# Gathering the rows of three experts instead of two in quarters of 128 columns, turned by VectorE, in a retention and mixture-of-experts kernel

## The chip, the core and the metric

The kernel runs on one core of a Trainium2 chip. The metric is the device time of one execution in microseconds. TensorE multiplies matrices, VectorE and ScalarE work element by element, GpSimd does so too and also starts the indirect transfers (gathers and scatters), SyncE starts the plain loads. Each engine takes its instructions in the order in which they were written and waits at semaphores for the others.

## What is computed

Retention (attention with a decay in place of the softmax) over 8 batches, 8 heads, 576 positions and 64 channels gives 4608 tokens of 512 channels. Every token goes to one of 8 experts, at most 576 tokens to each, chosen greedily by the logits; an expert is two products with a ReLU between.

```python
ret = (0.125 * q @ k.transpose(0, 1, 3, 2)) * Dmat      # gamma_h ** (i - j) for i >= j, else 0
x = (ret @ v).transpose(0, 2, 1, 3).reshape(4608, 512)
flat = (x @ w_gate).flatten()
for idx in np.argsort(-flat):
    tok, e = idx // 8, idx % 8
    if assigned[tok] >= 0 or counts[e] >= 576: continue
    assigned[tok] = e; counts[e] += 1
for e in range(8):
    out[assigned == e] = np.maximum(x[assigned == e] @ w1[e], 0) @ w2[e]
```

## The kernel before

**Stages.** The first 165 us or so are the retention; its rows go to a scratch tensor `xd` in HBM. Then eight experts follow. They are handled in the order in which they fill up: I call the expert that is found p-th "expert p", from 0 to 7, and `e` in the code of the products is that p. For an expert, TensorE runs the first product (`l1`, line 1041, PSUM tile `ph`) and the second (`l2`, line 1082, `py`). Every float32 operand is split in a high and a low part (`xh` and `xl`, `w1h` and `w1l`), and three of the four partial products are kept.

**The first product** has 16 steps: 8 blocks `f` of the hidden channels, each with the tokens 0 to 255 (12 products of 256 columns) and then the tokens 256 to 575 (12 products of 320 columns). So its first step needs the gathered blocks of tokens 0 and 1, and its second step needs blocks 2, 3 and 4, low parts too. **The second product** has five token blocks: four of 24 products of 512 columns, and a fifth of 64 tokens with 16. Three of those 24 (one `f`) I call a triple, two of the 16 a pair.

**Search and listing.** While TensorE works for expert p, VectorE looks for expert p+1 and then p+2 (class `Route`). A search has seven rounds; each is one count on TensorE (nine small products, line 353) and one stretch on VectorE that begins at line 357 and ends, with a new table `G` (line 177), before the next count. Then come `members` (counts of line 421) and `listing` (counts of line 459), which gives the indices of the rows in `idx` (line 471). Expert 7 needs no search.

**Gathering**, for expert e+1 while expert e is in work, is done in one of two ways, by the constant `PIECES`:

- For e < PIECES: five gathers of whole rows of 512 channels (line 975), four of 128 tokens and one of 64. TensorE turns each block with four transposes (line 1007) into PSUM, ScalarE copies out the high part (line 1009), VectorE subtracts for the low part (line 1010).
- For e >= PIECES: `listing` also makes the table `quarter` (lines 476 to 480, seven operations on VectorE), and 18 gathers follow (line 965), one for each of 128 indices, that fetch a quarter row of 128 channels. VectorE turns a block in place of TensorE (`xz`, line 991, two buffers), ScalarE copies out the high part (line 993), VectorE subtracts (line 994). The loader takes the weights of the first product from `w1n`, the same numbers in another order of channels, and four loads of 512 KB stay four loads of 512 KB.

```python
while left and (all or state['piece'] <= mix.t):
    k, v = left.pop(0)
    nc.gpsimd.indirect_dma_start(out=t[:, k, :], ..., ap=quarters[e][:, v:v+1], axis=0)
    state['piece'] = mix.t + 1300
if not left:
    XG[e] = t
    state['arrives'] = mix.t + 6000
```

**What sets the order.** A `Mixer` keeps a clock of its own, in nanoseconds, while the program is written: each triple of `l2` advances it by 650, each three products of `l1` by 320 or 400, and each stretch of VectorE by a fixed price. The next count of the search is written when that clock says that VectorE is done. `gather` writes a quarter gather every 1300 of that clock, and the turning of the blocks starts, one block for each triple, when `arrives` is over. So what stands behind what on each engine is decided here, when the program is built.

**GpSimd's queue** also holds, for each expert, eight transfers `w1l` and `w2l` (line 950), each of which forms the low part of a quarter of the weights in memory and waits for ScalarE's copy (line 949), and five scatters of results (line 1059). There is one buffer `xg` for gathered rows.

Of the kernel before, what the change touches and what calls it, by code (L numbers as in the profile page):

```python
# [19 lines left out]
NP, HP, NB = 4, 4, 9  # L20
N, DM, E, FF = 4608, 512, 8, 1024
SLACK = 1.0
PIECES = 6

def consts_np():
    h = np.arange(H); g = (1.0 - 2.0 ** (-5.0 - h)).astype(np.float64)
# [59 lines left out]
class Route:  # L86
# [341 lines left out]
    def listing(s, p):  # L428
# [43 lines left out]
        if early:  # L472
            s.room(cn)
        if p >= PIECES:
            s.quarter = pool.tile([128, 20], I32, name="quarter", bufs=2)
# [414 lines left out]
def moe(tc, nc, P, R, xd, w1_d, w2_d, out, mix):  # L890
# [11 lines left out]
    def phases():  # L902
        for p in range(E):
# [9 lines left out]
            found.append(R.idx)  # L913
            if p >= PIECES:
                quarters[p] = R.quarter
# [5 lines left out]
    def dma_pump():  # L921

        while state['dma'] < min(state['conv'] + 4, 8*E):
# [3 lines left out]
            t = P['raw']()  # L927
            src = ((w1_d[0] if e < PIECES else w1_d[1]) if k < 4 else w2_d)
            nc.sync.dma_start(t, src[bass.ds(regs[e], 1), :, (k % 4)*1024:(k % 4)*1024+1024].rearrange("a p x -> (a p) x"))
# [25 lines left out]
    def gather(e, all=False):  # L955
        if e in XG or not ready(e):
            return
        if e >= PIECES:
            if e not in parts:
# [20 lines left out]
    def transposes(e):  # L980
# [4 lines left out]
        XH[e], XL[e] = xh, xl  # L985
        if e >= PIECES:
            low = []
# [26 lines left out]
    def l1(e, tr):  # L1014
# [5 lines left out]
        for i, (f, s) in enumerate(order):  # L1020
            wh, wl = [w.rearrange("p (f d m) -> p f d m", f=2, d=4)[:, f % 2] for w in W1[e, f // 2]]
            if i == 0 and e >= PIECES:
                for _ in tr:
# [186 lines left out]
```

## Time and profile before

| | us |
|---|---|
| median of 3 runs | 625.21 (624.79 to 626.15) |
| the profiled execution | 626.64, of it the span 624.5 from the first to the last instruction |
| second product of expert 4 (the gathering for expert 5) | 429.70 to 459.41 |
| first and second product of expert 5 | 459.41 to 486.25 and 486.25 to 512.66 |
| first and second product of expert 6 | 512.66 to 538.3 and 538.3 to 563.8 |

All times inside the execution count from the first instruction. The products of TensorE overlap, so a row's duration is longer than the step from its start to the next row's start; what a group of products costs is read from the starts. A row of the timeline that ends in square brackets names the idle time ahead of the instruction and what ended it.

### The profile page before, as it was taken

The numbers are of one execution on the slowest core, as the hardware profiler recorded it, in microseconds if no ns is written. First come the engines' busy times: TensorE is split into PE (matmuls) and PEld (weight loads), VectorE is DVE, ScalarE is ACT, GpSimd is POOL, SyncE is SP. The second block draws the span as 40 slices with busy tenths as digits, with TensorE's granted clock in tenths as the row PEclk, the third lists the DMA queues.
The fourth block names the chain that finished last, engine by engine and source line by source line (L and its number), as shares of the span: only waits on it lengthen the run. The fifth ranks groups of instructions, "written<-read, shape, count | busy, mean of one in ns | idle before, by whom it ended". The sixth has DMA issues, their size and how long they took to land.

```text
span 624.5 us, 14777 instructions
## 1 busy us (share of the span) xinstructions
PE 600.9 (96%) x5718; PEld 518.3 (83%) x5722; DVE 406.7 (65%) x1487; ACT 270.5 (43%) x464; POOL 250.6 (40%) x297
## 2 busy tenths in 40 slices
PE   7999998998989999999999999999999999999993
PEld 5888887866589779978987997798789889989982
DVE  4646776698899878977885885689478632222200
ACT  1344432332347355542662456156435536645410
POOL 4887375410422262251242243124314868831121
PEclk9999998999999999999999999999999999999998
DMA  9999799954559699796889399559938887995410
GB/s 323 409 376 342 230 399 305 333 153 137 163 165 215 185 222 245 188 245 190 173 227 241 93 243 225 173 128 231 236 108 183 206 254 188 236 257 118 77 50 27
DMA packets 53352, 132.70 MB, mean 212 GB/s; under 512 B 7394, under 2 KB 22626, under 8 KB 53282
## 3 DMA queue, kind: packets, MB, share of 16 engines
q1 hardware_dynamic: 37906, 80.10, 37.7%
q0 software_dynamic: 15232, 51.39, 37.3%
q8 instruction: 45, 0.74, 0.5%
q10 hardware_dynamic: 144, 0.26, 0.1%
q14 instruction: 25, 0.20, 0.1%
HBM read 80.35 MB, written 18.87 MB: 159 GB/s over the span
## 4 chain that ended last, share of the span: by engine, by line
PE 75%; DVE 9%; DMA 7%; issue 6%; SPq 1%; POOL 1%; ACT 1%; POOLq 0%; DVEq 0%
PE py L1082 28%; PE ph L1041 28%; PE sc L603 4%; PE px L647 3%; DMA xd<-raw 3%; DMA vin<-in_vk 2%; PE px L638 2%; PE pS L624 2%; PE pt L1007 2%; PE r L353 1%; PE pT L679 1%; DVE hb L1048 1%; PE r L459 1%; DVE f L361 1%; DMA raw<-in_w 1%
## 5 line engine op out<-in xcount | busy, mean ns | idle before, releaser
L1082 PE MATMUL py<-w2h,hb 128*128 128x512 f32 x576 | 187.4, 397 | 0.0
L1041 PE MATMUL ph<-xh,w1h 128*128 128x320 f32 (+1 forms) x512 | 152.0, 301 | 0.2 <-ACT xh L1009 0.2
L1041 PE MATMUL ph<-xl,w1h 128*128 128x320 f32 (+1 forms) x512 | 149.7, 296 | 0.0
L1041 PE MATMUL ph<-xh,w1l 128*128 128x320 f32 (+1 forms) x512 | 149.5, 296 | 0.0
L1082 PE MATMUL py<-w2l,hb 128*128 128x512 f32 (+1 forms) x320 | 125.3, 392 | 0.0
L1082 PEld LDWEIGHTS py<-w2h,hb 128*128 128x128 f32 x576 | 104.4, 188 | 21.6
L1041 PEld LDWEIGHTS ph<-xh,w1h 128*128 128x128 f32 x512 | 96.3, 189 | 1.3 <-ACT xh L1009 0.7
L1041 PEld LDWEIGHTS ph<-xl,w1h 128*128 128x128 f32 x512 | 96.4, 190 | 0.2
L1041 PEld LDWEIGHTS ph<-xh,w1l 128*128 128x128 f32 x512 | 96.3, 189 | 0.0
L1045 ACT ACTIVATE hb<-ph 128x256 fp32r<-128x256 f32 (+1 forms) x128 | 52.2, 408 | 99.5 <-PE ph L1041 98.8
L1059 POOL DMA_INDIRECT out_y<-yt,idx x40 | 40.5, 1013 | 111.4 <-ACT yt L1099 73.0
L1048 DVE SCALAR_TENSOR_TENSOR hb<-ph,hb 128x256 fp32r<-128x256 f32 (+1 forms) x192 | 58.3, 352 | 40.0 <-ACT hb L1045 39.4
L1082 PEld LDWEIGHTS py<-w2l,hb 128*128 128x128 f32 (+1 forms) x320 | 56.7, 177 | 13.3 <-DMA w2l<-raw 0.4
L612 DVE TENSOR_TENSOR am<-sc,cst 128x1024 f32<-128x1024 f32 x32 | 39.1, 1223 | 37.5 <-PE sc L603 37.5
L588 POOL TENSOR_TENSOR qin<-qin,cst 128x512 f32<-128x512 f32 (+1 forms) x48 | 47.2, 1010 | 40.0 <-DMA qin<-in_qk 36.0
L950 POOL DMA_DIRECT2D w2l<-raw x32 | 29.4, 918 | 84.2 <-ACT w2l L949 44.4
L1099 ACT ACTIVATE yt<-py 128x512 f32<-128x512 f32 x32 | 19.1, 598 | 92.7 <-PE py L1082 73.5
L627 ACT ACTIVATE st<-pS,cst 128x128 f32<-128x128 f32 x64 | 23.5, 368 | 80.3 <-PE pS L624 80.3
L975 POOL DMA_INDIRECT xg<-xd,idx x30 | 30.0, 1000 | 68.7 <-DMA raw<-in_w 36.1
L950 POOL DMA_DIRECT2D w1l<-raw x30 | 28.0, 959 | 43.3 <-ACT w1l L949 36.1
L603 PE MATMUL sc<-qin,kin 64*128 64x128 f32 x512 | 39.9, 299 | 2.0 <-POOL qin L588 1.8
L965 POOL DMA_INDIRECT xg<-xd,quarter x36 | 36.3, 1008 | 12.8 <-issue 9.4
(192 smaller groups left out, 939.5 us busy)
## 6 DMA issues: line engine op xcount, KB each, us to landing
raw<-in_w SPq DMA_DIRECT2D x56, 512.0 KB, 6.1
w2l<-raw POOLq DMA_DIRECT2D x32, 512.0 KB, 6.0
w1l<-raw POOLq DMA_DIRECT2D x30, 512.0 KB, 7.2
qin<-in_qk SPq DMA_DIRECT2D x14, 576.0 KB, 6.6
kin<-in_qk SPq DMA_DIRECT2D x14, 576.0 KB, 7.0
vin<-in_vk SPq DMA_DIRECT2D x14, 576.0 KB, 9.2
nin<-in_vk SPq DMA_DIRECT2D x14, 512.0 KB, 8.7
xd<-raw SPq DMA_DIRECT2D x36, 128.0 KB, 6.4
```

The source lines that it names most:

```text
L588: nc.gpsimd.tensor_tensor(x, x, e[:, None, :n].to_broadcast([128, (b-a)//n, n]), op=ALU.mult)
L603: nc.tensor.matmul(t[:, h, 128*j:128*j+128], blk(k, 4*g+j)[r], blk(q, 4*g+j)[r], start=(j == 0), stop=True, skip_group_check=True)
L612: nc.vector.tensor_tensor(a, SC[u, g].rearrange("p h (j q) -> p h j q", q=128), m1[:, u % HP, :, None, :].to_broadcast([128, 2, 4, 128]), ...
L627: nc.scalar.activation(s, p, AF.Copy, scale=ss[:, u % HP, c:c+1])
L950: nc.gpsimd.dma_start(lo, raw, accum_op=ALU.add)
L965: nc.gpsimd.indirect_dma_start(out=t[:, k, :], out_offset=None, in_=xq[:, :], in_offset=bass.IndirectOffsetOnAxis(ap=quarters[e][:, v:v+1] ...
L975: nc.gpsimd.indirect_dma_start(out=xg[:n, j, :], out_offset=None, in_=xd[:, :], in_offset=bass.IndirectOffsetOnAxis(ap=found[e][:n, j:j+1] ...
L1041: T.matmul(ps, w, x, start=(k == 0), stop=(k == 11))
L1045: A.activation(hb[:, f, c], ps, AF.Relu)
L1048: V.scalar_tensor_tensor(hb[:, f, to+a:to+b], ps[:, a:b], 0.0, hb[:, f, 256*s+a:256*s+b].bitcast(F32), op0=ALU.max, op1=ALU.subtract)
L1059: st = nc.gpsimd.indirect_dma_start(out=out[:, :], out_offset=bass.IndirectOffsetOnAxis(ap=found[e][:n, t:t+1], axis=0), in_=y[:n], in_off ...
L1082: T.matmul(ps[:m], a, w, start=(k == 0), stop=(k == last), skip_group_check=True)
```

## The change

The constant goes from 6 to 5, so that expert 5 too is gathered in 18 quarter gathers and turned by VectorE; experts 6 and 7 were so already.

```diff
-PIECES = 6
+PIECES = 5
```

Twenty transposes of TensorE, five copies and five subtractions from PSUM go; seven operations on `quarter`, five turnings `xz`, five copies and five subtractions from SBUF come, and 18 gathers stand for 5. Since the mixer's clock sees other prices, other things move too.

On VectorE, at the end of the second product of expert 4 and the start of the first product of expert 5, the sixth round of the search for expert 6 stood before like this (`yt` is the last block of results of expert 4, `hb` the hidden layer of expert 5):

```order
L357 SCALAR_TENSOR_TENSOR cs<-room,r 32x8
L359 TENSOR_TENSOR cs<-cs,r 32x8 x2
L361 TENSOR_TENSOR f<-r,cs 32x8 x4
L367 TENSOR_REDUCE mq<-f 128x1
L368 STREAM_TRANSPOSE tc<-mq 128x32
L369 TENSOR_REDUCE j<-tc 128x1
L334 TENSOR_SCALAR v<-u,j 128x72
L177 TENSOR_TENSOR G<-ct,v 128x36x16
L1102 TENSOR_TENSOR yt<-yt,py 64x512
L1048 SCALAR_TENSOR_TENSOR hb<-ph,hb 128x256
```

and stands now like this (`xg` are the gathered rows of expert 5, the first row is the low part of block 2, the last two are those of blocks 3 and 4):

```order
L994 TENSOR_TENSOR xl<-xz,xh 128x4x128
L357 SCALAR_TENSOR_TENSOR cs<-room,r 32x8
L359 TENSOR_TENSOR cs<-cs,r 32x8 x2
L361 TENSOR_TENSOR f<-r,cs 32x8 x4
L367 TENSOR_REDUCE mq<-f 128x1
L368 STREAM_TRANSPOSE tc<-mq 128x32
L369 TENSOR_REDUCE j<-tc 128x1
L334 TENSOR_SCALAR v<-u,j 128x72
L177 TENSOR_TENSOR G<-ct,v 128x36x16
L991 STREAM_TRANSPOSE xz<-xg 128x4x64
L994 TENSOR_TENSOR xl<-xz,xh 128x4x128
L994 TENSOR_TENSOR xl<-xz,xh 128x4x64
```

The turning of expert 5's rows stands around that round: four of the five blocks ahead of it, the turning of the fifth block and two low parts behind it.

On GpSimd, in the second product of expert 5, the last gathers for expert 6 stood before like this:

```order
L965 DMA xg<-xd,quarter 128x128 x2
L950 DMA w1l<-raw 128x1024
L965 DMA xg<-xd,quarter 128x128 x2
L1058 MEMSET spacer_2326 1x1
L1059 DMA out_y<-yt,idx 4608x512
L965 DMA xg<-xd,quarter 128x128
L950 DMA w1l<-raw 128x1024
```

and stand now like this:

```order
L965 DMA xg<-xd,quarter 128x128 x2
L950 DMA w1l<-raw 128x1024
L965 DMA xg<-xd,quarter 128x128 x2
L1058 MEMSET spacer_2326 1x1
L1059 DMA out_y<-yt,idx 4608x512
L965 DMA xg<-xd,quarter 128x128
L950 DMA w1l<-raw 128x1024
L965 DMA xg<-xd,quarter 128x128 x3
```

The last two gathers, those of block 4, and the last of block 3 stand now behind the fourth `w1l`, which used to follow all of them.

On TensorE, the five groups of transposes between the first triples of the second product of expert 4 are gone. The listing counts for expert 6 (line 459) stand 27 products later in the first product of expert 5: 87 of its 192 products followed them before, 60 do now. The seventh count of that search stands after 30 products of it, where it stood after 15.

## Rows read from the trace of the kernel before

**Rows 1.** The page: busy time of each engine, share of the span, instructions

```profile
PE 600.9 (96%) x5718; PEld 518.3 (83%) x5722; DVE 406.7 (65%) x1487; ACT 270.5 (43%) x464; POOL 250.6 (40%) x297
```

**Rows 2.** Timeline of TensorE, second product of expert 4: start us, us, instruction

```profile
429.70 0.63 PE L1082 MATMUL py<-w2h,hb 128*128 128x512 f32 x2
...
437.65 0.39 PE L353 MATMUL r<-oh,G 128*128 128x32 bf16 x9
...
444.79 0.39 PE L353 MATMUL r<-oh,G 128*128 128x32 bf16 x9
...
449.91 0.39 PE L353 MATMUL r<-oh,G 128*128 128x32 bf16 x9
...
454.34 0.39 PE L353 MATMUL r<-oh,G 128*128 128x32 bf16 x9
...
459.41 0.27 PE L1041 MATMUL ph<-xh,w1h 128*128 128x256 f32 x1
...
460.83 0.31 PE L1041 MATMUL ph<-xh,w1h 128*128 128x320 f32 x1
```

**Rows 3.** Timeline of VectorE, same stretch: rounds five and six of the search

```profile
454.77 0.15 DVE L357 SCALAR_TENSOR_TENSOR cs<-room,r 32x8 f32<-32x8 f32 x1 [1.59 <-PE r L353]
...
457.40 0.19 DVE L345 TENSOR_TENSOR u<-v,D 128x36 f32<-128x36 bf16 x1
458.11 0.15 DVE L357 SCALAR_TENSOR_TENSOR cs<-room,r 32x8 f32<-32x8 f32 x1 [0.52 <-PE r L353]
...
460.36 0.46 DVE L177 TENSOR_TENSOR G<-ct,v 128x576 bf16<-128x576 bf16 x1
```

**Rows 4.** Timeline of VectorE: turning for expert 6 (its end), then for expert 7

```profile
512.74 0.45 DVE L991 STREAM_TRANSPOSE xz<-xg 128x256 f32<-128x256 f32 x1 [2.93 <-DMA xg<-xd,quarter]
513.11 0.98 DVE L994 TENSOR_TENSOR xl<-xz,xh 128x512 fp32r<-128x512 f32 x2
...
539.40 1.30 DVE L991 STREAM_TRANSPOSE xz<-xg 128x512 f32<-128x512 f32 x2
547.02 0.69 DVE L994 TENSOR_TENSOR xl<-xz,xh 128x512 fp32r<-128x512 f32 x1 [6.32 <-ACT xh L993]
...
550.39 0.45 DVE L991 STREAM_TRANSPOSE xz<-xg 128x256 f32<-128x256 f32 x1
```

**Rows 5.** Timeline of TensorE, experts 5 and 6: listing, second product, first product's two steps

```profile
473.73 0.85 PE L459 MATMUL r<-rh,G 128*128 128x160 bf16 x9
...
486.25 0.63 PE L1082 MATMUL py<-w2h,hb 128*128 128x512 f32 x2
...
512.66 0.28 PE L1041 MATMUL ph<-xh,w1h 128*128 128x256 f32 x1
...
514.08 0.31 PE L1041 MATMUL ph<-xh,w1h 128*128 128x320 f32 x1
```

**Rows 6.** Timeline of GpSimd: first gather for expert 5, gathers for expert 6

```profile
421.33 1.07 POOL L975 DMA_INDIRECT xg<-xd,idx  x1 [1.56 <-DVE room L494]
...
478.53 1.07 POOL L965 DMA_INDIRECT xg<-xd,quarter  x1 [2.20 <-DVE eb L504]
...
502.24 1.02 POOL L950 DMA_DIRECT2D w1l<-raw  x1
...
508.06 0.97 POOL L965 DMA_INDIRECT xg<-xd,quarter  x1 [0.31 <-issue]
```

**Rows 7.** TensorE after its two longest waits, then granted clock by stretch (PEclk)

```profile
100.84 1.19 PE L638 MATMUL px<-qin,st 64*64 64x128 f32 x24 [2.19 <-DVE at L616]
...
176.53 0.50 PE L1007 MATMUL pt<-ident,xg 64*128 64x64 f32 x4 [1.81 <-DVE xl L1010]
...
core 0: us, PE busy (x) PEld busy (x) DVE busy (x) ACT busy (x) POOL busy (x), PEclk, DMA share, GB/s
...
101.00:104.50 3.50, 3.50 (x50) 3.16 (x48) 1.76 (x7) 0.00 (x0) 2.15 (x2) 0.51 0.92 310
...
176.50:180.00 3.50, 2.89 (x29) 2.73 (x30) 3.02 (x14) 0.62 (x2) 0.00 (x0) 1.00 0.40 162
```

## The prediction

> **What bounds the kernel now.** I read the page first: TensorE is busy for 96% of the span [rows 1], so a change counts by what it takes off TensorE's path or makes TensorE wait for. Then the timeline of TensorE, from the second product of expert 4 to the first product of expert 6 [rows 2, 5]: the products follow each other without a wait. In the second product of expert 4 two counts with ten triples between them lie 7.14 us apart (437.65 to 444.79), with seven triples 5.12 (to 449.91), with six 4.43 (to 454.34); so a triple takes 0.68 and a count some 0.34. Then VectorE [rows 3, 4], which is the engine that inherits work, and GpSimd [rows 6]. In rows 3 the reader is to see how a round of the search hangs on its count: the round begins 0.43 after the count (454.34 and 454.77). In rows 4 and 5 he is to see how near the existing quarter gathers are to the edge: the last quarters for expert 6 landed at 512.74, VectorE waited for them, the low parts were done at 514.09 (513.11 and 0.98), and the second step of the first product began at 514.08, just in time.
>
> The change touches the stretch from 421 to the start of expert 6's first product. The sum is made against the profiled execution (626.64, span 624.5) and its difference is laid on the median of 625.21. I count 0.2% (1.25 us) as what a measurement here can tell from no change.
>
> **What it removes: 2.2 us of TensorE.** From 429.70 to 437.65 stand eight triples, one count and the five groups of transposes [rows 2]: 7.95 less 8 times 0.68 and 0.34 leaves 2.2. All of it lies on TensorE's path. Without them the second product of expert 4 ends at 457.2 instead of 459.41. The copies and subtractions that go and come on ScalarE and VectorE are alike in size; the seven operations on the index table, about 1.8 us on VectorE, come in the first product of expert 4, where VectorE serves a search whose first count is only due at 430.4; they cost nothing there as long as its first round's table is up by then (it was there 2 us earlier, by the same margin that the table eats up; between 0 and 0.3, I take 0).
>
> **What it adds on VectorE: a wait of 3.7 us.** The new order puts four turnings ahead of round six of the search and the fifth behind it, while the first product's second step needs the low parts of blocks 2, 3 and 4. Followed in order:
> - Count 1 stands after the first triple (430.4), counts 2 to 4 each seven triples later (5.12), so count 4 at 445.8; count 5 six triples later (4.43), at 450.2; count 6 sixteen products later, at 454.2; the end after twelve more, at 457.2.
> - Round five begins at 450.6 and takes 2.82 (454.77 to 457.59) [rows 3]: done at 453.4.
> - Two turnings take 1.30 [rows 4]; the first block's high part is copied beside the second turning, so its low part begins at about 454.8. For expert 7, from the first low part to the turning of the last block were 3.37 (547.02 to 550.39) [rows 4]. That point would be 458.2.
> - There stands round six instead, 2.71 long (458.11 to 460.82) [rows 3]. Then the last block's turning and two low parts, 1.35 (512.74 to 514.09) [rows 4]: 462.3.
> - TensorE's first step needs only blocks 0 and 1 (done at about 456.9) and takes 1.42 (459.41 to 460.83) [rows 2]: it is through at 458.6, and waits to 462.3.
>
> Are the gathers themselves in time? The first one went at 421.33 [rows 6]; with the index table 1.8 later, 423.2. For expert 6, 17 gathers and what stood between them took 29.53 to the 18th (478.53 to 508.06), and that one was usable 4.68 later (512.74) [rows 4, 6]. With the fourth `w1l` ahead of it (1.02, and about 0.3 to the next [rows 6]) the same would give 458.7, two us ahead of the turning that needs it (460.9). So the order on VectorE decides here, not the transfer; bounds of this wait are 2.4 (if the copies ran quite beside) and 5 (a gather as late as 462).
>
> **What it moves: the listing for expert 6, a wait of 4.8 us.** After the wait the second step begins at 462.3 where it began at 460.83. The listing counts of expert 6 now follow 132 products, not 105. From the second step on that is 120 products: ten steps at 1.42 for 256 columns and about 1.77 for 320, 16.0, and the other counts 0.5: 478.8 instead of 473.73 [rows 5]. 60 products remain instead of 87; 27 are 3.65, so the second product begins 12.52 less 3.65 after the listing, at 487.7 (486.25 before), and the first product of expert 6 another 26.41 later (486.25 to 512.66) [rows 5], at 514.1; its second step is due at 515.5.
> - The first gather went 4.80 after the listing (473.73 to 478.53): 483.6.
> - GpSimd's queue was full from there to the last gather: 29.53 for 17 gathers, one `w2l`, three `w1l` and two scatters [rows 6]. Now a fourth `w1l` stands ahead of the last: 30.8, so the 18th goes at 514.4, is usable 4.68 later, at 519.1, and the low parts are done 1.35 later, at 520.4.
> - So TensorE waits from 515.5 to about 520.3: 4.8. It had no wait there before, since listing and gathers were just in time; every us by which the listing falls back against the end of the product is paid. Bounds: 2.3 and 7.
>
> The first gather for expert 7 follows the scatters of expert 5 and moves by the same amount; its turning was through at about 551.7, 12 us ahead of its use at 563.8, so nothing more comes there.
>
> At this place a rule of the Trainium skill gives another sum. DMA: Bandwidth & Descriptors, section "Anatomy of one DMA — SWDGE (gpsimd) path", fits one transfer at 2.0 us and its bytes by 436 KB a us. A quarter gather of 64 KB would so land after 2.15 us, an estimate from that page, and the wait would be 2.5 us shorter, the sum 632.0. The trace disagrees (4.68) [rows 4, 6], and it decides.
>
> **What the waits do to the clock: 3 us.** The one wait of TensorE above 2 us in the running kernel, 2.19 us before 100.84, was followed by a granted clock of 0.51 from 101.0 to 104.5, that is the lower of the two levels, 1.2 GHz; after the wait of 1.81 before 176.53 it stayed at 1.00 [rows 7]. 3.5 us at half speed lose 1.7. Both new waits are longer than 2.19. Part of the slow stretch can fall into the wait itself, so I take 1.5 for each, with 0 and 2.5 as bounds. Listing, gathers and products after the first wait shift together, so the 4.8 stay.
>
> The rule behind this is in the Trainium skill, TensorE: Matmul & The Clock Gate, section "HAM oscillation — how this bites in real kernels": waits between bursts of matmuls throttle the array, and the next burst starts slow. It speaks against this change; by the rule both waits are charged (634.5), by the 1.81 us row alone neither (631.5).
>
> **Sum.** Less 2.2, plus 3.7, plus 4.8, is 6.3; with 3.0 for the clock 9.3. On the median: 625.2 + 9.3 = 634.5.
>
> **The rivals.**
> - *No fall of the clock.* For it: the wait of 1.81 us [rows 7]. Against it: that of 2.19. It gives 631.5. Chance 0.15.
> - *Only the first wait.* If the gathers for expert 6 make up the 4.8 us on GpSimd or land sooner, 625.2 - 2.2 + 3.7 + 1.5 = 628.2. Against it: GpSimd's queue had no gap to give (29.53 us for 23 entries, about 1.28 each). Chance 0.10.
> - *The transfers land by the page's fit.* 632.0, chance 0.03.
> - *A further wait*, most likely gathers that land later in a fuller queue: 3 us more, 637.5 or above. Chance 0.05.
> - *Faster.* The 2.2 us stay and neither wait comes: 623.0. This needs VectorE to be through with block 4 by 458.6, that is without round six ahead of it, and the last quarter for expert 6 to be usable by about 514; from a total of 2.2 us of waits on, it is no gain. For it: the same way of gathering runs for experts 6 and 7 without a wait of TensorE [rows 4, 5]. Against it: those have no search rounds on VectorE beside them. Chance 0.04.
> - That the change doesn't do what it says can be put aside: the order of the instructions shows it.
>
> **How the numbers follow.** The forecast, 632 to 637 around 634.5, has 0.61. With the cases above: slower by over 0.2% 0.94, within 0.2% 0.02 (smaller waits that eat up the 2.2 and no more), faster 0.04. The range takes in the single wait at the low end and the bounds of the clock and the gathers at the high end: 628 to 638.
>
> **What would show it.** Right: in the second product of expert 4 no transposes, its end about 457; a wait of TensorE of about 3.7 us after twelve products of the next first product, ended by `xl` (line 994); the listing about 5 us later; VectorE's turning of the last block of expert 6 waiting for a gather, and a second wait of TensorE of 4 to 5 us at the same place; a clock near 0.5 for a few us after each; from expert 7 on everything as before, shifted. Wrong: no wait ended by line 994, or a last gather for expert 6 that is usable before 515.

## The result, and the profile after the change

The changed kernel takes 633.88 us (median of 6 runs, 631.53 to 636.93), beside 625.89 for the kernel before in the same comparison: ratio 1.0104, interval 1.0069 to 1.0140, so 4.3 to 8.8 us slower. The forecast was 634.5, with 628 to 638 as its range.

The profiled execution of the changed kernel is its slowest one (636.93, span 635.2), 10.7 us longer in its span than that of before. Where do these 10.7 us lie? Timeline of TensorE, the rows that answer to [rows 2] and [rows 5] (start us, us, instruction; in brackets the idle time ahead of it and what ended it):

```profile
433.30 0.63 PE L1082 MATMUL py<-w2h,hb 128*128 128x512 f32 x2
...
461.02 0.28 PE L1041 MATMUL ph<-xh,w1h 128*128 128x256 f32 x1
...
465.41 0.41 PE L1041 MATMUL ph<-xh,w1h 128*128 128x320 f32 x1 [2.79 <-ACT xh L993]
465.87 0.42 PE L1041 MATMUL ph<-xl,w1h 128*128 128x320 f32 x1
...
483.81 0.85 PE L459 MATMUL r<-rh,G 128*128 128x160 bf16 x9
...
492.77 0.62 PE L1082 MATMUL py<-w2h,hb 128*128 128x512 f32 x2
...
519.17 0.28 PE L1041 MATMUL ph<-xh,w1h 128*128 128x256 f32 x1
...
524.74 0.64 PE L1041 MATMUL ph<-xh,w1h 128*128 128x320 f32 x1 [3.99 <-ACT xh L993]
```

Take the differences between starts. The second product of expert 4 lasts 27.72 (29.71 before), the first product of expert 5 31.75 (26.84), its second product 26.40 (26.41), the first product of expert 6 31.29 (25.60). That is -1.99, +4.91, 0, +5.69, together +8.6. The first row stands 3.60 later than in [rows 2], though TensorE has the same work up to there and the product just ahead of it takes 26.84 (26.85 before): that is chance of the execution (below). And the last 1.5 us of the difference are won back behind the last product, where nothing was forecast: from the start of the last scatter to the end are 7.84 before, 6.34 now.

The two waits are where they were looked for. Each first product's second step is due 1.42 after its first step. Expert 5: due 462.44, begun 465.41 with the high part, the first product with the low part at 465.87: 3.0 to 3.3 late. Expert 6: due 520.59, begun 524.74: 4.15 late. VectorE at both places (the rows of [rows 3] and [rows 4]):

```profile
461.84 0.15 DVE L357 SCALAR_TENSOR_TENSOR cs<-room,r 32x8 f32<-32x8 f32 x1
...
464.10 0.46 DVE L177 TENSOR_TENSOR G<-ct,v 128x576 bf16<-128x576 bf16 x1
464.47 0.44 DVE L991 STREAM_TRANSPOSE xz<-xg 128x256 f32<-128x256 f32 x1
464.83 0.98 DVE L994 TENSOR_TENSOR xl<-xz,xh 128x512 fp32r<-128x512 f32 x2
...
518.23 0.65 DVE L994 TENSOR_TENSOR xl<-xz,xh 128x512 fp32r<-128x512 f32 x1
522.48 0.71 DVE L991 STREAM_TRANSPOSE xz<-xg 128x512 f32<-128x512 f32 x1 [3.60 <-issue]
523.11 0.65 DVE L994 TENSOR_TENSOR xl<-xz,xh 128x512 fp32r<-128x512 f32 x1
523.80 0.45 DVE L991 STREAM_TRANSPOSE xz<-xg 128x256 f32<-128x256 f32 x1
524.16 0.99 DVE L994 TENSOR_TENSOR xl<-xz,xh 128x512 fp32r<-128x512 f32 x2
```

At the first place round six (461.84 to 464.56) runs in one piece with the turning, without a gap. At the second VectorE stands idle for 3.60 ahead of block 3, and block 4 follows without a gap. GpSimd says why (the rows of [rows 6]): the fourth `w1l`, and behind it the last gather of block 3 and the two of block 4. The first row is the last gather for expert 5, the second the first one for expert 6.

```profile
457.64 1.05 POOL L965 DMA_INDIRECT xg<-xd,quarter  x1 [0.31 <-issue]
...
488.63 1.07 POOL L965 DMA_INDIRECT xg<-xd,quarter  x1 [5.77 <-DVE eb L504]
...
514.67 1.01 POOL L950 DMA_DIRECT2D w1l<-raw  x1
515.98 1.05 POOL L965 DMA_INDIRECT xg<-xd,quarter  x1 [0.30 <-issue]
517.34 1.07 POOL L965 DMA_INDIRECT xg<-xd,quarter  x1 [0.30 <-issue]
518.71 0.99 POOL L965 DMA_INDIRECT xg<-xd,quarter  x1 [0.30 <-issue]
```

Block 3 was turned 6.5 us after its last gather was issued (515.98 to 522.48). This profile names no releaser for the 3.60; in e5, which has the same order, the wait at the same place (2.95) is ended by the gather (`xg<-xd,quarter`).

Behind both waits TensorE runs at the lower of its two levels, 1.2 GHz (the granted clock stands behind the count in round brackets; 1.00 is 2.4 GHz, 0.50 is 1.2):

```profile
core 0: us, PE busy (x), PEclk, DMA share, GB/s
433.30:461.00 27.70, 27.69 (x168) 1.00 0.88 212
...
467.00:468.00 1.00, 1.00 (x5) 0.50 0.08 16
...
470.00:472.00 2.00, 2.00 (x23) 1.00 0.00 0
...
524.70:525.70 1.00, 0.96 (x3) 0.50 0.47 188
...
528.00:529.00 1.00, 1.00 (x10) 1.00 0.31 66
```

### The profile page after: what moved, and what is told of

Its sections match the earlier page's. It is cut to its first block, busy times and chain, and to the rows that moved or that the text cites. A ratio compares the mean times of both kernels' runs of the same rounds, so it can differ in the third digit from the quotient of the medians.

```text
span 635.2 us, 14769 instructions
## 1 busy us (share of the span) xinstructions
PE 603.2 (95%) x5702; PEld 520.1 (82%) x5702; DVE 410.4 (65%) x1500; ACT 270.4 (43%) x464; POOL 265.9 (42%) x310
## 4 chain that ended last, share of the span: by engine, by line
PE 66%; DMA 11%; DVE 8%; issue 8%; SPq 2%; ACT 2%; POOL 1%; POOLq 0%; DVEq 0%; ACTq 0%
PE ph L1041 30%; PE py L1082 24%; DMA vin<-in_vk 5%; DMA xd<-raw 2%; PE sc L603 2%; PE px L647 2%; DMA raw<-in_w 2%; PE r L353 1%; PE pS L624 1%; PE px L638 1%; PE pt L1007 1%; DMA nin<-in_vk 1%; DMA qin<-in_qk 1%; SPq L708 1%; SPq L558 1%
## 5 line engine op out<-in xcount | busy, mean ns | idle before, releaser
L1041 PE MATMUL ph<-xh,w1h 128*128 128x320 f32 (+1 forms) x512 | 154.2, 305 | 7.0 <-ACT xh L993 6.8
L1041 PE MATMUL ph<-xl,w1h 128*128 128x320 f32 (+1 forms) x512 | 151.6, 300 | 0.0
L1041 PE MATMUL ph<-xh,w1l 128*128 128x320 f32 (+1 forms) x512 | 151.4, 300 | 0.0
L1041 PEld LDWEIGHTS ph<-xh,w1h 128*128 128x128 f32 x512 | 97.9, 193 | 8.4 <-ACT xh L993 7.2
L1041 PEld LDWEIGHTS ph<-xl,w1h 128*128 128x128 f32 x512 | 98.0, 193 | 0.7 <-DVE xl L994 0.4
L1041 PEld LDWEIGHTS ph<-xh,w1l 128*128 128x128 f32 x512 | 98.2, 193 | 0.0
L965 POOL DMA_INDIRECT xg<-xd,quarter x54 | 55.1, 1021 | 24.9 <-issue 15.8
L975 POOL DMA_INDIRECT xg<-xd,idx x25 | 25.2, 1009 | 64.7 <-DMA raw<-in_w 36.1
```

Of the source, the lines that this page charges most:

```text
L965: nc.gpsimd.indirect_dma_start(out=t[:, k, :], out_offset=None, in_=xq[:, :], in_offset=bass.IndirectOffsetOnAxis(ap=quarters[e][:, v:v+1] ...
L975: nc.gpsimd.indirect_dma_start(out=xg[:n, j, :], out_offset=None, in_=xd[:, :], in_offset=bass.IndirectOffsetOnAxis(ap=found[e][:n, j:j+1] ...
L1041: T.matmul(ps, w, x, start=(k == 0), stop=(k == 11))
```

## How the experiments are read

The start of the second product of expert 4 lies between 427.85 and 436.26 in the profiles. All kernels have the same code up to the first product of expert 4, and that product takes 26.83 to 26.85 in each of them; one and the same kernel gave 433.25 and 427.85 (e9, e11), another 432.67 and 430.61 (e4, e8). So beside the times, which hold that chance, each profile's **stretch** is given: from that start to the start of the first product of expert 7, which holds all that the change moves on TensorE. Two profiles of one kernel agree in it within 0.6 to 1.4. "End" is from the start of the last scatter to the last instruction.

| | us (median) | before beside it | ratio (95% interval) | stretch | end |
|---|---|---|---|---|---|
| before | | | | 134.05 | 7.84 |
| changed | 633.88 | 625.89 | 1.0104 (1.0069 to 1.0140) | 142.65 | 6.34 |
| e1 | 632.77 | 626.67 | 1.0089 (1.0061 to 1.0118) | 139.07 | 7.81 |
| e2 | 627.76 | 627.37 | 1.0003 (0.9972 to 1.0034) | 136.19 | 6.77 |
| e3 | 631.86 | 626.67 | 1.0083 (1.0050 to 1.0116) | 141.56 | 6.31 |
| e4 | 626.81 | 626.67 | 1.0006 (0.9981 to 1.0031) | 137.93 | 6.30 |
| e8 (e4 again) | 629.49 | 627.37 | 1.0032 (1.0004 to 1.0059) | 137.30 | 6.28 |
| e5 | 631.06 | 626.67 | 1.0067 (1.0045 to 1.0089) | 139.50 | 6.36 |
| e6 | 636.16 | 627.37 | 1.0116 (1.0068 to 1.0164) | 142.73 | 6.30 |
| e7 | 631.45 | 627.37 | 1.0049 (1.0018 to 1.0080) | 138.20 | 7.85 |
| e9 | 627.79 | 627.82 | 1.0011 (0.9980 to 1.0043) | 138.31 | 6.33 |
| e11 (e9 again) | 628.58 | 628.13 | 1.0025 (0.9993 to 1.0056) | 139.70 | 6.34 |
| e12 | 624.37 | 627.01 | 0.9942 (0.9919 to 0.9965) | 134.94 | 6.36 |
| e13 (e12 again) | 628.70 | 627.44 | 1.0021 (0.9988 to 1.0054) | 135.84 | 6.29 |

For the changed kernel stretch and end together give +8.6 - 1.5 = +7.1, inside its interval of 4.3 to 8.8 us.

## The price of the transposes: e2

```diff
-PIECES = 5
+PIECES = (7,)          # and e in PIECES where e >= PIECES stood
```

> Quarter gathers and turning by VectorE for expert 7 alone; expert 6 too goes back to whole rows and transposes on TensorE. It prices the twenty transposes in a second product without anything else: the listing stands where it stood before. My theory: the second product of expert 5 takes 2.2 us longer (26.41 to 28.6), nothing else changes, and the stretch from the second product of expert 4 to the first of expert 7 is 136.3 (134.05 before): 2 us slower. Rival (the transposes hide beside other work, or the whole-row gathers come too late): less than 1, or 3 and more with a wait on the gathered rows ahead of a transpose.

The second product of expert 5, which had no transposes before, now has them (timeline of TensorE; the last row is the first product of expert 6):

```profile
488.57 0.39 PE L1082 MATMUL py<-w2h,hb 128*128 128x512 f32 x1
...
489.34 0.52 PE L1007 MATMUL pt<-ident,xg 128*128 128x128 f32 x4
...
517.15 0.28 PE L1041 MATMUL ph<-xh,w1h 128*128 128x256 f32 x1
```

It takes 28.58 where it took 26.41: twenty transposes cost 2.17, and all of the stretch's +2.14 is that. The end is 1.07 shorter, so that the time hardly shows it. The first theory holds. The change itself took away 1.99 in its own profile and 2.14 or 2.15 in e1, e3 and e5, which have the same order there; the difference is a pause of 0.17 of TensorE in its own profile, ahead of the second count of the search (439.27).

## Each wait by itself: e1, e4, e3

**e1: expert 5 as changed, expert 6 by transposes.**

```diff
-PIECES = 5
+PIECES = (5, 7)        # and e in PIECES where e >= PIECES stood
```

> Quarter gathers and turning by VectorE for experts 5 and 7; expert 6 goes back to whole rows and transposes on TensorE. The order around expert 5 is that of the changed kernel. My theory (each wait has its own cause: the first the turning of expert 5 around search round six, the second the late quarter gathers for expert 6): the transposes of the second product of expert 4 stay gone (-2.0), the first wait stays (3.0 to 3.3, ended by line 993 or 994 in the first product of expert 5) with its slow clock (+1.6), the transposes for expert 6 come back on TensorE (+2.2), and no wait of 4 us stands in the first product of expert 6: 4 to 6 us above the kernel before, about 631. Rival (the second wait is a late effect of the first, whatever way expert 6 is gathered, since everything behind the first wait is late): a wait of about 4 us stands in the first product of expert 6 here too, ended by the copies of line 1009, and the time is 635 or more.

```profile
465.56 0.63 PE L1041 MATMUL ph<-xh,w1h 128*128 128x320 f32 x1 [2.79 <-ACT xh L993]
```

The first wait is the same to the digit, and the first product of expert 6 takes 25.58, that is no wait at all. The stretch is 5.0 longer than before; the terms of the theory add up to 4.8 to 5.1. The second wait is no late effect of the first, it needs the quarter gathers for expert 6.

**e4: the listing early.** The mixer's clock charges nothing for the turning of expert 5.

```diff
-                mix.vec(700)
+                mix.vec(700 if e != 5 else 0)
...
-                    mix.vec(610)
+                    mix.vec(610 if e != 5 else 0)
```

> The changed kernel without the price that the mixer's clock charges for the turning of expert 5, so that the listing for expert 6 comes early: its counts stand after 90 of the 192 products (132 in the changed kernel, 105 before), and the last gathers for expert 6 stand ahead of the fourth w1l. The order of turning and round six on VectorE stays; the seventh count of the search now stands ahead of the first product of expert 5 and waits there for round six. My theory (the late listing makes the second wait): no wait in the first product of expert 6; the first wait stays, 3 us, now ahead of the first product's first step and ended by the table G (line 177), with its slow clock: 628 to 630, some 5 us below the changed kernel. Rival (quarter gathers for expert 6 are slow whenever a second set of quarter gathers precedes them, or the transfers collide with others): the second wait stays at 3 us or more and the time is 632 or above.

```profile
512.25 1.02 POOL L965 DMA_INDIRECT xg<-xd,quarter  x1 [0.30 <-issue]
...
514.62 0.99 POOL L950 DMA_DIRECT2D w1l<-raw  x1
...
516.69 0.45 DVE L991 STREAM_TRANSPOSE xz<-xg 128x256 f32<-128x256 f32 x1 [1.63 <-DMA xg<-xd,quarter]
```

The last gather for expert 6 now goes ahead of the fourth `w1l`, is usable at 516.69, 2.8 us ahead of the first product of expert 6 (519.52), and that takes 25.59: the second wait is gone with the late listing. The first one stays, one step earlier:

```profile
463.83 0.42 PE L353 MATMUL r<-oh,G 128*128 128x32 bf16 x9 [3.43 <-DVE G L177]
```

Its clock cost more here: 0.50 from 464.1 to about 469.5, 5.4 us, where it was some 3.4 in the changed kernel. The times lay far apart (622.85 to 631.6), so it was run again:

> The same kernel as the changed one without the price of the turning, once more: its first profile had a wait of 3.43 us ahead of the first product of expert 5, 5.4 us at half clock behind it, and a stretch of 137.93 us from the second product of expert 4 to the first product of expert 7, but its times lay apart (622.85 to 631.6). If the clock falls behind a wait of this length every time, the profile again shows a clock of 0.50 behind the wait and a stretch of 137.9; if it falls only sometimes, the clock can stay at 1.00 there and the stretch is 135 to 136. What lies ahead of the second product of expert 4 is the same code in all kernels; if the times lie apart because of that part, the stretch is 137.9 in both and the start of that product moves by 3 us or so.

The wait is 3.43 again, the clock falls again, for about 3.4 us this time; the stretch is 137.30. The median, 629.49, lies in the 628 to 630 that was expected of the first run, whose own 626.81 lay below it. So what lay apart is mostly the part ahead of the stretch, and a wait of this length cost half of 3.4 to 5.4 us each time, 1.7 to 2.7.

**e3: all of expert 5 turned ahead of round six.**

```diff
-                yield
+                if e != 5: yield
```

> The changed kernel with all five blocks of expert 5 turned in one go, so that on VectorE search round six stands behind the last turning and the last two low parts. Listing and gathers for expert 6 stand where they stood in the changed kernel. My theory (the order on VectorE makes the first wait): the second step of expert 5's first product begins when the last gather has landed and its block is turned. That gather was issued at 457.64 and had landed by 464.47 in the changed kernel; 4.7 us after the issue would be 462.3, with 1.4 for turning and low parts 463.7, where the step is due at 462.4: a wait of 1 to 2 us in place of 3.0, and no fall of the clock behind it. Round six then ends about 1.5 us later, its count stands after 39 products in place of 30 and waits at most 0.6. The second wait (4.2, with its slow clock) stays. Together 2 to 3 us below the changed kernel, 631 to 632. Rival (the transfers decide the first wait): the last gather lands at 464 or later, the wait is 3 us or more as before, the clock falls, and the time is 634 or above.

Timeline of GpSimd (the last gather), VectorE and TensorE:

```profile
458.61 1.05 POOL L965 DMA_INDIRECT xg<-xd,quarter  x1 [0.30 <-issue]
...
465.08 0.45 DVE L991 STREAM_TRANSPOSE xz<-xg 128x256 f32<-128x256 f32 x1 [2.20 <-DMA xg<-xd,quarter]
465.45 0.98 DVE L994 TENSOR_TENSOR xl<-xz,xh 128x512 fp32r<-128x512 f32 x2
...
466.03 0.41 PE L1041 MATMUL ph<-xh,w1h 128*128 128x320 f32 x1 [2.34 <-ACT xh L993]
```

The time, 631.86, came as expected, but the theory is wrong by half. VectorE is free at 462.9 and has to wait for the last gather till 465.08, 6.47 after its issue. The wait of TensorE shrinks from 2.79 to 2.34 only, and the clock falls all the same (0.50 from 467.0 to 470.0). So the first wait has two causes that end within half a microsecond of each other: round six in the way, and a last gather that lands no sooner (6.47 behind its issue at 457.64 in the changed kernel would be 464.11, where round six ended at 464.56). Taking away one of them gains next to nothing.

## The price of the clock: e5

```diff
-            xh, xl = XH[e], XL[e]
+            xh, xl = XH[e], XL[e]; warm({5: 14, 6: 18}[e]) if i == 1 and e in (5, 6) else None
```

> The changed kernel with idle matmuls of 512 columns (bf16, of a constant; 14 and 18 of them, about 3.1 and 4.0 us) put on TensorE between the first and the second step of the first products of experts 5 and 6, where it waits anyway. Nothing else moves. My theory (behind each wait about 1.5 us are lost to the clock): the granted clock stays near 1.00 behind both places and the second steps run at full speed: 2.5 to 3.3 us below the changed kernel, about 631. Rival (the products behind the waits are slow for want of operands, or the clock's price is small): no gain, 633.5 to 635.

```profile
459.95 3.20 PE L1163 MATMUL warm<-full 128*128 128x512 bf16 x14
462.90 0.41 PE L1041 MATMUL ph<-xh,w1h 128*128 128x320 f32 x1
...
core 0: us, PE busy (x), PEclk, DMA share, GB/s
...
464.00:466.00 2.00, 2.00 (x23) 1.00 0.07 16
...
522.00:524.00 2.00, 2.00 (x18) 1.00 0.30 70
```

Busy with matmuls that nobody needs, TensorE keeps 1.00 through both waits. The first products take 30.21 and 29.83 in place of 31.75 and 31.29: 1.54 and 1.46. Nothing else in the stretch differs by more than the 0.15 of the pause named above, so 3.0 us of the change's loss are the clock's. The theory holds (2.5 to 3.3), its rival falls.

## Can the turning be had without the waits? e6, e7, e9, e11, e12, e13

If e1 to e5 are right, an order in which round six is out of the way, the last gather for expert 5 goes earlier and the listing is not later than before should keep the 2 us. A first try:

```diff
-            mix.slack = 1.0 if p < 2 else 1.2 if p < 4 else 1.35
+            mix.slack = 1.0 if p < 2 else 1.2 if p < 4 else 1.35 if p < 6 else 1.0
...
-                state['piece'] = mix.t + 1300
+                state['piece'] = mix.t + 1000
...
-                yield
+                if e != 5: yield
+                elif j == 4: mix.vec(3000)
```

> The changed kernel with four numbers of the order set anew, so that both causes of the first wait and that of the second go: the search for expert 6 is paced with slack 1.0 in place of 1.35, so that rounds five and six stand ahead of all turning; quarter gathers are written every 1000 of the mixer's clock in place of 1300, so that one w1l, one scatter fewer stand ahead of the last gather for expert 5 (two entries of GpSimd, some 2.7 us); the five blocks are turned in one go, with 3000 charged behind them. The listing counts for expert 6 then stand after 87 products of expert 5's first product (132 in the changed kernel, 105 before). My theory: measured from the start of the second product of expert 4, the last gather is issued at 21.4 (24.1 with all blocks turned ahead of round six), is usable 6.5 later at 27.9, and the low parts are done at 29.3, where the second step is due at 29.3: a wait of at most 1 us, no fall of the clock, no wait in the first product of expert 6. The stretch from there to the first product of expert 7 is 132 to 133 us (134.05 before, 142.65 with the change), 1 to 2 us faster than the kernel before: 624.5 to 625.5 beside a kernel before at 626.5. Rival (rounds at slack 1.0 are too tight, so that TensorE waits at the search's counts, or the count of line 421 waits for round seven): waits of 1 to 3 us at lines 353 or 421, and 627 or above.

The waits of its rival came: 1.08 and 4.12 at the search's counts, 1.03 at line 421, and one of 2.14 for a `w2l` of expert 6, which the denser gathers had probably pushed back. The rival's reason is not shown for the longest: ahead of the 4.12 VectorE stood still for 4.92, which comes up again below. The control, the kernel before with the same two numbers:

> The kernel before (quarters for experts 6 and 7 only, transposes for expert 5 on TensorE) with the same two numbers for the search's slack (1.0 for expert 6) and the pace of quarter gathers (1000): the control for the run with the order set anew. My theory (TensorE is busy throughout, so an earlier search gives nothing by itself): within 1 us of the kernel before, and the stretch from the second product of expert 4 to the first of expert 7 is 134 us. Rival (the two numbers are what gains): the stretch is 1 us or more shorter.

This one I had wrong: 4.15 longer in the stretch. An earlier search is no gift; with the counts so close, TensorE waits 1.16 and 1.45 at line 421 for `sc`, which VectorE has not ready. These are 2.6 of the 4.15, a wait for a `w2l` is 0.39 more; the rest was not followed. A milder order, e9:

```diff
-            mix.slack = 1.0 if p < 2 else 1.2 if p < 4 else 1.35
+            mix.slack = 1.0 if p < 2 else 1.2 if p < 4 else 1.35 if p < 6 else 1.1
...
-                state['piece'] = mix.t + 1300
+                state['piece'] = mix.t + {5: 1000, 6: 1150}.get(e, 1300)
...
-                yield
-            low.pop(0)()
+                if e != 5: yield
+            low.pop(0)(); mix.vec(2500 if e == 5 else 0)
```

> The changed kernel with the order around expert 5 set anew a second time, with milder numbers: slack 1.1 for the search for expert 6 (counts of the search after 3, 21, 39, 57, 72 and 87 products, the first ones as far apart as before), quarter gathers for expert 5 every 1000 and for expert 6 every 1150 of the mixer's clock, expert 7 as before (1300), all five blocks of expert 5 turned in one go right behind round five, 2500 charged behind them. Round six and its count follow (30 products into expert 5's first product), the listing counts stand after 105 products, where they stood before the change, and all gathers for expert 6 ahead of its fourth w1l. My theory (with the last gather early and the turning ahead of round six both waits go): the last gather for expert 5 is issued 21.1 after the start of the second product of expert 4 and usable at 27.6, the low parts are done at 29.0, the second step is due at 29.0: a wait of at most 1; the seventh count waits at most 0.5; no wait in the first product of expert 6; the clock stays up. The stretch from the second product of expert 4 to the first of expert 7 is 132 to 134.5 us (134.05 before, 142.65 with the change), and the time within 2 us of the kernel before, on the fast side. Rival (what is taken from one wait comes back as another, since VectorE has rounds, turning and the emptying of the hidden layer to do at the same time): waits of 1 us or more at lines 353, 421 or 1041, a fall of the clock, and a stretch of 136 or more.

Both old waits are gone: no wait at either second step, 25.59 for the first product of expert 6. But a new one stands at the third count of the search, and the clock falls behind it. It was run again:

> The same kernel as that with the search ahead and the turning behind round five, once more. In its first profile both waits at the first products were gone, but a wait of 3.37 us stood at the third count of the search: VectorE and ScalarE both stood still for 4.8 us and more from 439.0 to 443.8, with no releaser that the profile knows. If that standstill belongs to the order (dense gathers), it is there again, the stretch from the second product of expert 4 to the first of expert 7 is 138 again, and the kernel is no faster than the one before. If it was of that one execution (which was the second slowest of twelve), it is gone, the wait at the third count is below 0.5, and the stretch is 132.5 to 134 (134.05 before): the turning by VectorE is then worth up to 1.5 us once its waits are out of the way.

Timelines of VectorE, ScalarE and TensorE in the second profile (the first shows the same):

```profile
433.56 0.39 PE L353 MATMUL r<-oh,G 128*128 128x32 bf16 x9 [0.43 <-DVE G L177]
...
438.44 0.15 DVE L357 SCALAR_TENSOR_TENSOR cs<-room,r 32x8 f32<-32x8 f32 x1 [4.83 <-remote]
...
438.54 0.60 ACT L1099 ACTIVATE yt<-py 128x512 f32<-128x512 f32 x1 [6.26 <-issue]
...
441.53 0.42 PE L353 MATMUL r<-oh,G 128*128 128x32 bf16 x9 [3.39 <-DVE G L177]
```

VectorE's round needs only the count, which ended at 433.95; it begins at 438.44, and ScalarE moves again at the same moment. The profile knows no releaser. In e6 and in both runs of this order the standstill of VectorE is 4.92, 4.82 and 4.83 long. The next kernel changes the order on GpSimd alone, where one gather falls behind a `w1l`; the other engines have the same instructions in the same order:

```diff
-                state['piece'] = mix.t + {5: 1000, 6: 1150}.get(e, 1300)
+                state['piece'] = mix.t + {5: 1150, 6: 1150}.get(e, 1300)
```

> The kernel with the search ahead once more, with the quarter gathers for expert 5 every 1150 of the mixer's clock in place of 1000. TensorE, VectorE, ScalarE and SyncE have the very same instructions in the same order; on GpSimd one gather fewer stands ahead of the first w1l for expert 5, and so one gather each falls behind the next w1l and scatters; the last one goes about 1.3 us later (22.4 after the start of the second product of expert 4). In the two profiles at 1000, VectorE and ScalarE stood still for 4.8 us in the second round of the search. If that standstill hangs on the order of GpSimd's transfers, it is gone or elsewhere: the wait of 3.4 us at the third count goes, the last gather is usable at 27 to 29 and the low parts are done at 28.4 to 30.4, a wait of 0 to 1.4 at the second step, and the stretch from the second product of expert 4 to the first of expert 7 is 132.5 to 134.5 (134.05 before): within 1 us of the kernel before or faster. If it hangs on VectorE's own order (rounds at slack 1.1), it is there again: a wait of 3.4 at the third count and a stretch of 138 to 140.

```profile
438.05 0.15 DVE L357 SCALAR_TENSOR_TENSOR cs<-room,r 32x8 f32<-32x8 f32 x1 [0.38 <-PE r L353]
...
460.86 0.45 DVE L991 STREAM_TRANSPOSE xz<-xg 128x256 f32<-128x256 f32 x1 [2.56 <-issue]
...
461.81 0.41 PE L1041 MATMUL ph<-xh,w1h 128*128 128x320 f32 x1
```

No standstill, no wait above 0.7 at a count, the second step 0.3 late, the clock at 1.00 all along, and 2.6 us faster than the kernel before by the medians, 2.2 to 5.1 by the interval of the ratio. But the stretch is 0.9 longer than before and the end 1.5 shorter, 0.6 less together; the profile shows no source for the rest. It was run once more, on another chip:

> The kernel with the search ahead and the gathers of expert 5 at 1150 once more, which was faster than the kernel before (624.37 to 627.01). Its profile, of the slowest of its twelve executions, had no wait at the first products, but small ones elsewhere (0.42 at the second count, 0.41 and 0.67 at line 421), a stretch of 134.94 us from the second product of expert 4 to the first of expert 7 (134.05 before), and 1.5 us less from the start of the last second product to the end, as all kernels with quarters for experts 5, 6 and 7 have (33.7 in place of 35.2). If stretch and end are the same in each execution, they make 0.6 us less than before, and the rest of the 2.6 is chance of the stages ahead of the change: then the ratio comes out at 0.997 or above this time. If the gain is the order's, the stretch comes out at 133 or less and the ratio again at 0.996 or below.

```profile
441.26 0.15 DVE L357 SCALAR_TENSOR_TENSOR cs<-room,r 32x8 f32<-32x8 f32 x1 [3.55 <-remote]
...
444.35 0.39 PE L353 MATMUL r<-oh,G 128*128 128x32 bf16 x9 [2.10 <-DVE G L177]
```

There the standstill is back, 3.55 long, and the gain is gone (1.0021, as expected if the 2.6 were mostly chance). So the standstill does not hang on GpSimd's order alone. What it is stays open; while it does, this kernel is level with the one before, not proven better. What is shown is narrower: with round six and the late gather both out of the way the first wait goes (e12; in e9, e11 and e13 TensorE came later to that place, behind the standstill, so that they show less), with the listing at its old place the second, and behind both places the clock stays up.

## Why the prediction was right, point by point

- **Less 2.2 for the transposes**: 1.99, 2.14 or 2.15 without the pause at the second count (e1, e3, e5), and 2.17 the other way round (e2).
- **First wait, 3.7**: 3.0 to 3.3. The low parts were forecast for 462.3 and were done at 465.81, 462.2 without the 3.60 by which this execution runs late. So the path on VectorE came out to 0.1. The wait is shorter for two reasons: the end of the second product before it came 0.2 later than forecast (457.4), by the pause at the second count, and TensorE began the second step with the high part of block 4 (`xh`, line 993), 0.46 ahead of the first product that needs the low part. The forecast had the wait end with `xl`, line 994, and named a wait that does not end there as a sign of being wrong; both waits end with line 993, so by the letter that sign came, while the mechanism, the late turning, held.
- **"The order on VectorE decides here, not the transfer"**: true by 0.4 us, where the text had 2. The last gather went as forecast (454.0), but needed 6.5 us to be usable (e3) and not the 4.68 of [rows 4, 6]. This was the step on the thinnest ground: one duration, of one gather, taken for another place. Better rows stood in the trace of the kernel before. Of its gathers for expert 6, those issued directly behind a 512 KB transfer of GpSimd landed after 6.6 (483.48), 6.1 (491.17), 5.9 (496.08) and 4.9 (503.56); the 18th, which gave the 4.68, had two gathers and a scatter in between and landed after 4.6. In the changed kernel the last gather for expert 5 stands directly behind a `w1l`, and so does the last of block 3. The Trainium skill, DMA: Bandwidth & Descriptors, section "Anatomy of one DMA — SWDGE (gpsimd) path", gives 2.15 by its fit, an estimate. The trace disagrees here (4.4 to 6.5 for the gathers that VectorE waited for); only the shortest landing of a quarter gather in the kernel before, 2.5 (481.21), comes near it.
- **Second wait, 4.8**: 4.15. Its cause is settled by e4 and e1: the late listing, in quarters only. Inside it two errors met: against the first product's start the last gather went 0.8 earlier than forecast (0.46 ahead of it, where 0.3 behind it was put), and it was block 3's gather, not block 4's, that came last, again by a longer transfer (6.5).
- **Clock, 3.0**: 1.54 and 1.46 (e5). The rival without a fall of the clock is out. The Trainium skill, TensorE: Matmul & The Clock Gate, section "HAM oscillation — how this bites in real kernels", has the array throttled by waits between bursts of matmuls; the trace agrees at both places (0.50 behind 2.79 and 3.99). The two rows on which the forecast rested, 2.19 with a fall and 1.81 without, were thin ground all the same: the changed kernel has a fall behind a wait of 1.87 (last section).
- **Only the first wait**, **faster**: the first would have needed the gathers for expert 6 ahead of the fourth `w1l` (e4), the second also no round in the way and an earlier last gather for expert 5, as in e12; and even that kernel is not proven faster. *A further wait* did not come: besides the two, TensorE has none of 0.3 or more in the stretch.
- **What the sum left out**: the 1.5 us at the end. With it the 8.6 become 7.1, still inside the interval; no view of the kernel before that was read hinted at it.
- **Where the number was lucky**: 633.88 lies 0.6 from 634.5, but the kernel before measured 0.7 more beside it than the 625.21 of the forecast. The forecast rise of 9.3 stands against 8.0 by the medians and 6.5 by the ratio: both waits were put somewhat too long, and the end was left out.

## What to carry to other kernels

Work that is taken off the busiest engine has to be followed to the queue that inherits it: here 2 us of TensorE were paid with 7 us of waits, because VectorE had search rounds and GpSimd transfers standing in the way. Before removing a wait, ask what ends just behind the thing that you remove; two causes half a microsecond apart need two changes. And price a wait of the matmul engine with its clock: here some 1.5 us more for each of the two.

## What was not expected of the hardware

- **Landing of a quarter gather** (128 rows of 512 bytes, issue to first use by a VectorE that waits for it): 4.4 (e4), 5.3 (e8), 5.9 (e5, block 3), 6.1 (e12), 6.5 (e3, and block 3 in the changed kernel). The place in GpSimd's queue goes with it: directly behind a 512 KB transfer stood those of 5.9 (e5) and 6.5, one gather further back those of 4.4 and 5.3. It is not all: the 6.1 of e12 had two gathers and a scatter in between. One number from one place is no constant.
- **The clock behind waits of TensorE**: in the stretch it stayed at 1.00 behind 2.10 (e13) and 2.14 (e6), and was at 0.50 behind 2.34 and 3.41 (e3), 2.79, 3.37 (e9), 3.39 (e11), 3.43 (e4, e8), 3.99 and 4.12 (e6), for 3 to 5.9 us of work. Ahead of the stretch the length of a wait alone does not decide: the clock stayed at 1.00 behind 2.30 (e4, 122.84) and 2.58 (e9, 209.60), and in the changed kernel it was at 0.50 from 179.7 to 182.4, behind a wait of 1.87 that ended at 177.11. So 1.81 and 2.19 [rows 7] are no boundary.
- **The end**: 7.8 from the last scatter to the last instruction with two experts in quarters (before, e1, e7), 6.8 with one (e2), 6.3 with three (the changed kernel and the nine other runs). The last scatter moves the same 0.13 MB in the kernel before and in the changed one; the cause of the shorter end was not tried.
- **The standstill** of VectorE and ScalarE in four profiles (e6, e9, e11 and e13; not in e12, which is e13's kernel): 3.55 to 4.92 us on VectorE, without a releaser that the profile knows. Open. The chips differ too: e12 ran on one, e11 and e13 on a second, e6 and e9 on two others.
